# Bias rows of the first four heads made in their own partitions, and six early loads moved from GpSimd's queue to SyncE's

## The chip, the cores and the metric

The kernel runs on one core of a Trainium2 chip (the chip has eight). The metric is the device time of one execution in microseconds (us), the median of several runs. Five engines work side by side, each through its own list of instructions in order: TensorE (PE in the profile, with its weight loads as PEld), VectorE (DVE), ScalarE (ACT), GpSimd (POOL) and SyncE (SP). They wait for one another through semaphores. SP, ACT and POOL can issue DMA transfers; an engine that issues one spends time on the issue, and the transfer lands later.

## The reference, cut to what matters

Attention over 8 batches of 8 heads (64 heads, called head 0 to 63 here), 576 positions and head dimension 64, with a causal mask and a bias made of running sums of `s`; its output is the input of a gated feed-forward block.

```python
scores = scale * np.matmul(q, k.transpose(0, 1, 3, 2))
s_pos = np.maximum(s, 0.0)
cum = np.cumsum(s_pos, axis=-1)
bias = -(cum[:, :, :, None] - cum[:, :, None, :])
scores = np.where(causal, -1000000000.0, scores + np.minimum(bias, 0.0))
...                                   # softmax, then attn @ v gives x
g = x @ w_gate
silu = g * (1.0 / (1.0 + np.exp(-g)))
return (silu * (x @ w_val) @ w_out)   # 4608 tokens, 512 -> 1536 -> 512
```

The bias of position i against position j is `cum[j] - cum[i]`: a product of a column with ones. The kernel adds it inside the score product: beside the 64 rows of head dimension, an operand has extra rows that hold the running sum (in two parts, high and low, so that two 16-bit numbers carry it) and constants.

## The kernel before, in words

**Operands.** Four heads make a block (`HB`); block 0 is heads 0 to 3, block 1 heads 4 to 7. For a block there are two tiles `KQ[i][r]` (`kq` in the profile; `i` is the block modulo 2, `r` picks the pair of heads), 128 partitions by 2 sides (0 is q, 1 is k) by two heads of 576 columns and 64 columns of padding. For `r = 0`, partitions 0 to 63 hold the transposed head data and partitions 64 to 67 the bias rows, the rest of that half being zero; for `r = 1` the halves are swapped.

**Bias rows.** SP loads all 64 rows of `s` into `s_sb` (L188). DVE clips and scales it (L226), makes the running sum `c8` by a scan (L227), rounds it to 16 bits as the high part (L230), subtracts to get the low part (L231), and copies both parts for the other side (L232); the constant rows of the tile `HL` are filled by two memsets (L200, L201). `HL` has a partition for each head. The function `aug` (L183) then moves a head's four rows from its one partition of `HL` to four partitions of `kq` by a DMA, a DMA for each head, issued by SP for blocks 0 to 3.

**Head data.** `load_one` (L140) loads k or q as float32 (`rawk`, `rawq`); block 0 in two halves (`r = 0`, `r = 1`) by SP, blocks 1 and 2 whole by POOL. A cast to 16 bits (`ck`, `cq`) follows: L254 on ACT or L256 on POOL for the halves of block 0, L246 on DVE for block 1 and on POOL for block 2. PE transposes the cast data into a PSUM bank (L301 for halves, L287 for whole blocks), and L314 (ACT) or L316 (DVE) copies it from the bank to `kq`. V of batch 0 is loaded in five chunks by POOL (L157, `rawv`) and cast by POOL (four chunks, L168) and DVE (the last).

**Order of the start.** It is written out by hand at the end of the kernel and scheduled manually: each engine does its instructions in the order of the program text. `keep_warm` (L884) is a row of PE products whose result nobody reads: 32 at the start, 10 after the transposes of `r = 0`, 10 after those of `r = 1`. Then comes, in PE's order:

```python
        scores(0)
        half_batch("k")
        scores(1)
        half_batch("q")
        scores(2)
        scores(3)
```

`scores(h)` is `score_piece` for the four column chunks of head h: PE adds a mask product for the masked chunks (L353, `lower`) and the score products (L359), and ACT takes the exponential (L369) from the bank into `pt`. `half_batch(nm)` is the nine transposes (L287) of block 1's k or q, and the first four copies (L316) to `kq`. PE takes its products strictly in this order, so the products of head 1 stand behind the transposes of block 1's k, and those behind the cast of block 1's k.

**Banks.** PSUM has eight banks, handed out by `take` in a rotation fixed when the program is built; a product that opens a bank waits until the engine that read the bank last is done. The first piece of head 1 goes into bank 4, from which the last part of block 0's q (`r = 1`) is copied before.

**Later.** Heads 4 to 7, the products of the probabilities with V (L396, `values`), and then a loop over nine tiles of 512 tokens: gate and value products (L630), the down projection (L687, or by seven products instead of eight, L736), with the attention of the next batch pumped in between.

Of the kernel before, what the change touches and what calls it, by code (L numbers as in the profile page):

```python
# [12 lines left out]
FP32 = mybir.dt.float32  # L13
BF16 = mybir.dt.bfloat16
AF = mybir.ActivationFunctionType
ALU = mybir.AluOpType
# [3 lines left out]
def kernel(  # L20
# [43 lines left out]
    def pt_col(tj, bi):  # L64
# [4 lines left out]
    const = ctx.enter_context(tc.tile_pool(name="const", bufs=1))  # L69
# [21 lines left out]
    KQ = [  # L91
        [const.tile([128, 2, NR * S + 64], BF16, name=f"kq{e}{i}") for e in range(2)]
        for i in range(2)
    ]
    VT = [const.tile([128, NCH, H, D + 1], BF16, name=f"vt{i}") for i in range(2)]
    ident = const.tile([128, 128], BF16)
    one_s = const.tile([128, 1], FP32)
    HL = const.tile([BH, 4, 2, S], BF16)
    XR = 3 * TT
    XT = const.tile([128, 4, XR], BF16)  # L100
    warm = const.tile([128, 1], FP32)
    WS = const.tile([128, NFT // 2, 3, DM // 2], BF16)
    first_sbuf = ExitStack()
    first = first_sbuf.enter_context(tc.tile_pool(name="first", bufs=1))
    s_sb = first.tile([BH, S], FP32)
    c8 = first.tile([BH, S], FP32)
    PTP = {0: first, "bufs": 7}
    lower = first.tile([128, 512], BF16)

    with tc.manual_schedule():  # L110
# [50 lines left out]

        def cast_v(b, c, eng):
            n = 128 if c < 4 else TAIL
            dst, src_t = VT[b % 2][0:n, c, :, 0:D], loaded["v", b][0:n, c, :, :]
            if eng is nc.scalar:
                nc.scalar.copy(dst, src_t)
            else:
                eng.tensor_copy(dst, src_t)  # L168

        ONES2 = 1.0019378662109375  # L170
# [3 lines left out]
        def aug_rows(i, r):  # L174
            r0 = 64 * (1 - r)
            return KQ[i][r][r0 : r0 + 64, :, :].bitcast(FP32)

        def aug(hb, engs):
            for hh in range(HB):
                r, e = divmod(hh, 2)  # L180
                r0 = 64 * (1 - r)
                bh = hb * HB + hh
                engs[hh].dma_start(  # L183
                    KQ[hb % 2][r][r0 : r0 + 4, :, e * S : (e + 1) * S],
                    HL[bh : bh + 1, :, :, :],
                )
# [12 lines left out]
        nc.scalar.activation(warm, warm, AF.Exp)  # L199
        nc.vector.memset(HL[:, 0:2, 0, :].bitcast(FP32), ONES2)  # L200
        nc.vector.memset(HL[:, 2:4, 1, :].bitcast(FP32), NEGS2)  # L201
        make_identity(nc, ident)
        nc.gpsimd.memset(lower, 0.0)
        nc.gpsimd.affine_select(
# [3 lines left out]

        def pads(i):
            for r in range(2):  # L210
                nc.gpsimd.memset(KQ[i][r][64 * r : 64 * r + 64, :, NR * S :], 0.0)

        for r in range(2):
            nc.gpsimd.memset(aug_rows(0, r)[:, 1, :], 0.0)
# [4 lines left out]
        pads(0)  # L219
        nc.vector.memset(aug_rows(1, 0), 0.0)  # L220
        for nm in ("k", "q"):
            load_one(1, nm, eng=nc.gpsimd)
        init_vt(0)
        pads(1)

        nc.vector.tensor_scalar(s_sb, s_sb, 0.0, 8.0, ALU.max, ALU.mult)  # L226
        nc.vector.tensor_tensor_scan(  # L227
            c8, one_s[0:BH, 0:1].to_broadcast([BH, S]), s_sb, 0.0, ALU.mult, ALU.add
        )
        nc.vector.tensor_copy(HL[:, 0, 1, :], c8)  # L230
        nc.vector.tensor_sub(HL[:, 1, 1, :], c8, HL[:, 0, 1, :])  # L231
        nc.vector.tensor_copy(HL[:, 2:4, 0, :], HL[:, 0:2, 1, :])  # L232

        SP4 = [nc.sync] * 4
        GP4 = [nc.gpsimd] * 4
# [3 lines left out]
        def cast_one(hb, name, eng):  # L239
            cts[name, hb] = cp.tile([128, J, NR, D], BF16, tag="c" + name, bufs=2, name="c" + name)  # L240
            dst = cts[name, hb].rearrange("x j r d -> x r j d")
            src_t = loaded[name, hb]
            if eng is nc.scalar:
                nc.scalar.copy(dst, src_t)
            else:
                eng.tensor_copy(dst, src_t)  # L246

        def cast_half(hb, name, r, eng):
            if r == 0:
                cts[name, hb] = cp.tile([128, J, NR, D], BF16, tag="c" + name, bufs=2, name="c" + name)  # L250
            dst = cts[name, hb][:, :, r, :]
            src_t = loaded[name, hb][:, r, :, :]
            if eng is nc.scalar:
                nc.scalar.copy(dst, src_t)  # L254
            else:
                eng.tensor_copy(dst, src_t)  # L256
# [47 lines left out]

        def pe_out(hb, name, g, r, eng):
            j0, j1 = JG[g]
            kq = SRC[name][1]
            dst = KQ[hb % 2][r][64 * r : 64 * r + 64, kq, 0 : NR * S].rearrange(
                "a (x j) -> a x j", j=J
            )[:, :, j0:j1]  # L310
            tp = tps[name, g]
            srcp = tp[0][64 * r : 64 * r + 64].rearrange("a j x -> a x j")
            if eng is nc.scalar:
                nc.scalar.copy(dst, srcp)  # L314
            else:
                eng.tensor_copy(dst, srcp)  # L316
            tp[2] -= 1
            if tp[2] == 0:
                give(tp[1])
# [566 lines left out]
        def row_half(nm, r, eng):  # L886
            for g in range(2):
                pe_transpose_half(0, nm, g, r)
            for g in range(2):
                pe_out(0, nm, g, r, eng)  # L890

        def half_batch(nm):
            for g in range(2):
# [36 lines left out]
        w_load("v", 0, 1)  # L930
        for nm in ("g", "v"):
# [134 lines left out]
```

## Time and profile before

| what | us |
|---|---|
| median of three runs (376.23 to 377.41) | 376.51 |
| span of the profiled execution, first to last instruction | 375.9 |
| that execution's own time, its span with what lies around it: shown only through the runs | 376.23 to 377.41, so 0.3 to 1.5 around the span |
| PE busy | 364.4 (97%) |
| DVE busy | 290.4 (77%) |
| ACT busy | 240.3 (64%) |
| POOL busy | 212.1 (56%) |
| first score product (L359) | 12.65 |
| first exponential (L369) | 13.08 |

The mean granted PE clock is 1.000 over the span, and the clock row of the page shows 9 (90% or more) in each slice. By stages the PE is busy for 13.93 of the first 20 us, 38.82 of the next 40, and 311.67 of the last 315.9.

In the rows of the timeline the first number is the start in us from the span's start, the second the time that the merged instructions took, then engine, line, operation, what is written and what is read, shapes, and the count. A bracket gives the idle time before, and what ended it. In the rows by group the numbers behind the bar are the busy time in us, the mean in ns, and the idle time of the engine before them.

### The profile page before, as it was taken

How to read it: one execution, taken by the hardware profiler on the slowest of the kernel's cores; microseconds unless marked ns; L12 is line 12 of the kernel's file. 1: busy time of each engine (PE TensorE's matmuls, PEld its weight loads, DVE VectorE, ACT ScalarE, POOL GpSimd, SP SyncE). 2: the span in 40 equal slices, each digit the busy share in tenths (PEclk: the TensorE clock that was granted, in tenths of full speed). 3: DMA queues.
4: the chain of work that ended last, by engine and by line, in shares of the span. 5: the costliest groups of instructions: out<-in, count | busy, mean ns of one | idle time of the engine just before them, and what ended most of it. 6: DMA issues, size and time to landing. Idle time of an engine off the chain costs nothing.

```text
span 375.9 us, 8800 instructions
## 1 busy us (share of the span) xinstructions
PE 364.4 (97%) x3300; PEld 231.1 (61%) x3300; DVE 290.4 (77%) x578; ACT 240.3 (64%) x471; POOL 212.1 (56%) x325
## 2 busy tenths in 40 slices
PE   7699999999999999999999999999999999999995
PEld 6475556655555556855685558655865585476464
DVE  8867867458995899679976997599858867975984
ACT  8687777597986887578757876687465523323321
POOL 8982556665365657494649555955675416315320
PEclk9999999999999999999999999999999999999999
DMA  7899999799599998796869665995132103002003
GB/s 237 197 267 265 201 248 272 216 312 242 169 185 267 246 255 221 168 275 217 224 145 262 192 162 163 264 188 145 39 104 77 35 19 127 2 0 90 24 0 113
DMA packets 97146, 64.23 MB, mean 171 GB/s; under 512 B 77232, under 2 KB 82736, under 8 KB 97104
## 3 DMA queue, kind: packets, MB, share of 16 engines
q1 hardware_dynamic: 84976, 41.46, 45.9%
q0 software_dynamic: 12128, 22.21, 22.6%
q8 instruction: 26, 0.43, 0.5%
q14 instruction: 16, 0.13, 0.1%
HBM read 37.90 MB, written 19.86 MB: 154 GB/s over the span
## 4 chain that ended last, share of the span: by engine, by line
PE 90%; POOL 3%; ACT 2%; DVE 2%; DMA 1%; issue 1%; DVEq 0%; POOLq 0%; ACTq 0%
PE bank L630 47%; PE bank L736 17%; PE bank L359 11%; PE bank L396 8%; PE bank L687 6%; ACT pt L369 2%; DMA kq<-HL 1%; DVE kq L316 1%; PE bank L446 1%; DVE pp L653 1%; PE bank L287 1%; POOL vt L168 1%; DVE ht L664 1%; PE bank L353 1%; ACT kq L314 0%
## 5 line engine op out<-in xcount | busy, mean ns | idle before, releaser
L369 ACT ACTIVATE pt<-bank 128x512 bf16<-128x512 f32 (+1 forms) x256 | 120.3, 510 | 32.1 <-PE bank L359 18.9
L630 PE MATMUL bank<-XT,wg 128*128 128x512 bf16 x432 | 111.4, 379 | 0.5 <-DVE pp L653 0.3
L630 PE MATMUL bank<-XT,wv 128*128 128x512 bf16 x432 | 110.9, 379 | 0.1
L651 ACT ACTIVATE th<-bank 128x512 bf16<-128x512 f32 x108 | 64.7, 599 | 55.7 <-PE bank L630 51.1
L653 DVE SCALAR_TENSOR_TENSOR pp<-th,bank 128x512 bf16<-128x512 bf16 x108 | 73.7, 682 | 18.7 <-ACT th L651 18.2
L664 DVE SCALAR_TENSOR_TENSOR ht<-pp,bank 128x512 bf16<-128x512 bf16 x108 | 74.1, 687 | 10.6 <-PE bank L630 0.4
L359 PE MATMUL bank<-kq 128*128 128x128 bf16 (+4 forms) x576 | 75.8, 240 | 2.7 <-DMA kq<-HL 2.3
L673 POOL TENSOR_TENSOR ht<-ht 128x512 bf16<-128x512 bf16 x35 | 40.4, 1155 | 52.3 <-DVE su L671 52.2
L359 PEld LDWEIGHTS <-kq 128*128 128x128 bf16 x576 | 45.8, 98 | 33.1 <-DMA kq<-HL 2.6
L630 PEld LDWEIGHTS <-wv 128*128 128x128 bf16 x432 | 38.4, 98 | 36.4 <-issue 0.6
L630 PEld LDWEIGHTS <-wg 128*128 128x128 bf16 x432 | 38.3, 98 | 34.2 <-issue 0.7
L374 POOL TENSOR_SCALAR_AFFINE_SELECT pt<-pt 128x512 bf16<-128x512 bf16 x56 | 37.0, 661 | 30.8 <-ACT pt L369 23.4
L396 PEld LDWEIGHTS <-pt 128*128 128x128 bf16 x960 | 41.7, 98 | 17.3
L396 PE MATMUL bank<-vt,pt 128*128 128x65 bf16 x960 | 46.9, 194 | 0.3 <-POOL vt L168 0.3
L430 POOL DMA_DIRECT2D xs<-ot x24 | 21.7, 904 | 30.0 <-DVE ot L413 27.7
L736 PEld LDWEIGHTS <-ht 128*128 128x128 bf16 x336 | 31.2, 98 | 4.3
L413 DVE TENSOR_TENSOR ot<-bank,rc 128x320 bf16<-128x320 f32 x64 | 31.5, 492 | 2.2
L183 POOL DMA_DIRECT2D kq<-HL x48 | 28.7, 599 | 0.0
L687 PE MATMUL bank<-wo,ht 128*128 128x512 bf16 x96 | 25.8, 379 | 0.0
L736 PEld LDWEIGHTS <-su 128*128 128x128 bf16 x252 | 23.6, 98 | 3.3
L412 DVE RECIPROCAL rc<-bank 128x5 f32<-128x5 f32 x64 | 12.1, 189 | 15.3 <-PE bank L396 14.8
L801 POOL TENSOR_TENSOR ysb<-ysb 128x512 f32<-128x512 f32 x12 | 15.2, 1271 | 15.3 <-DVE ysb L795 15.3
(93 smaller groups left out, 389.1 us busy)
## 6 DMA issues: line engine op xcount, KB each, us to landing
out_dram<-ysb POOLq DMA_DIRECT2D x32, 256.0 KB, 3.9
rawv<-in_v_dram SPq DMA_DIRECT2D x28, 256.0 KB
rawk<-in_k_dram SPq DMA_DIRECT2D x12, 576.0 KB
rawq<-in_q_dram SPq DMA_DIRECT2D x12, 576.0 KB
xs<-ot POOLq DMA_DIRECT2D x24, 160.0 KB, 4.0
ks<-ck SPq DMA_DIRECT2D x11, 288.0 KB
qs<-cq SPq DMA_DIRECT2D x11, 288.0 KB
rawk<-in_k_dram POOLq DMA_DIRECT2D x3, 576.0 KB, 6.8
```

The source lines that it names most:

```text
L359: nc.tensor.matmul(sc[:, o : o + w], T[:, 1, e * S + 128 * tj : e * S + 128 * (tj + 1)], T[:, 0, e * S + lo : e * S + hi], start=not maske ...
L369: nc.scalar.activation(pt[:, c0 : c0 + n], sc, AF.Exp, scale=0.125)
L374: nc.gpsimd.affine_select(pt[:, 1088:1600], pt[:, 1088:1600], pattern=[[0, 4], [1, 128]], compare_op=ALU.is_ge, fill=zreg, base=0, channel ...
L396: nc.tensor.matmul(av[:, bi * (D + 1) : (bi + 1) * (D + 1)], pt[:, c0 : c0 + 128], VT[b % 2][:, tj, h, :], start=(tj == 0), stop=(tj == bi),)
L413: nc.vector.tensor_mul(ot[:, :, e * D : (e + 1) * D], av3[:, :, 0:D], rc[:, :, None].to_broadcast([128, NCH, D]),)
L630: nc.tensor.matmul(view(bs, TT), w[:, c, f0 : f0 + 128], xt[:, c, :], start=(c == 0), stop=(c == 3),)
L651: nc.scalar.activation(th, pg, AF.Tanh, scale=0.5)
L653: nc.vector.scalar_tensor_tensor(pp, in0=th, scalar=1.0, in1=pg, op0=ALU.add, op1=ALU.mult)
L664: nc.vector.scalar_tensor_tensor(hp[:, 2 * k2 : 2 * k2 + 2, :].rearrange("p a n -> p (a n)"), in0=pp, scalar=0.5, in1=pv, op0=ALU.mult, op ...
L673: (nc.vector if ft == NFT - 1 else nc.gpsimd).tensor_sub(hp[:, 1:3, :], hp[:, 1:4:2, :], hp[:, 0:3:2, :])
L687: nc.tensor.matmul(view(pys[ts_], DM), hps[ft // 2][:, 2 * (ft % 2) + half, c0 : c0 + 128], WO[j][:, ft % WKO, :], start=(ft == 0), stop=( ...
L736: nc.tensor.matmul(ps, lhs(p), rhs(p), start=(first and p == 0), stop=(last and p == NP - 1), skip_group_check=True,)
```

## The change

Diff, cut to its core. `...` marks what is left out.

```diff
-    HL = const.tile([BH, 4, 2, S], BF16)
+    HL = const.tile([128, 4, 2, S], BF16)
...
-    s_sb = first.tile([BH, S], FP32)
-    c8 = first.tile([BH, S], FP32)
+    s_sb = first.tile([128, S], FP32)
+    c8 = first.tile([128, S], FP32)
+    rows8 = first.tile([128, 8], FP32)
+    roles = first.tile([128, 4], FP32)
...
+        def hl_row(bh):
+            return bh + 4 if bh < 60 else bh + 64
...
-        nc.sync.dma_start(s_sb, s.rearrange("b h n -> (b h) n"))
+        s_copies(0, nc.sync)
+        s_copies(1, nc.scalar)
+        nc.scalar.dma_start(s_sb[8:64, :], s_rows[4:60, :])
+        nc.scalar.dma_start(s_sb[72:128, :], s_rows[8:64, :])
...
             load_one(0, "q", (r, r + 1))
+        load_qk(1)
...
-            nc.scalar.mul(
-                KQ[0][r][64 * (1 - r) : 64 * (1 - r) + 64, 0, :],
-                one_s[0:64, 0:1].to_broadcast([64, NR * S + 64]), 0.0,
-            )
...
-        for nm in ("k", "q"):
-            load_one(1, nm, eng=nc.gpsimd)
...
+        nc.vector.tensor_add(rows8, ident[:, 0:8], ident[:, 64:72])
+        nc.vector.tensor_add(roles, rows8[:, 0:4], rows8[:, 4:8])
+        nc.vector.tensor_reduce(a_q, roles[:, 0:2], axis=mybir.AxisListType.X, op=ALU.add, negate=True)
+        nc.vector.tensor_add(a_k, roles[:, 2:3], roles[:, 3:4])
+        nc.vector.tensor_reduce(b_lo, rows8[:, 0:4], axis=mybir.AxisListType.X, op=ALU.add)
+        nc.vector.tensor_scalar_add(b_lo, b_lo, -1.0)
...
         nc.vector.tensor_copy(HL[:, 0, 1, :], c8)
-        nc.vector.tensor_sub(HL[:, 1, 1, :], c8, HL[:, 0, 1, :])
-        nc.vector.tensor_copy(HL[:, 2:4, 0, :], HL[:, 0:2, 1, :])
+        nc.vector.scalar_tensor_tensor(
+            HL[:, 1, 1, :], in0=HL[:, 0, 1, :], scalar=b_lo, in1=c8,
+            op0=ALU.mult, op1=ALU.add,
+        )
+
+        def sums_rows(r, e, eng):
+            r0 = 64 * (1 - r)
+            for side, a, m in ((1, a_k, e), (0, a_q, 2 + e)):
+                eng.tensor_scalar(
+                    KQ[0][r][r0 : r0 + 64, side, e * S : (e + 1) * S],
+                    HL[r0 : r0 + 64, 1, 1, :], a[r0 : r0 + 64, :],
+                    roles[r0 : r0 + 64, m : m + 1], ALU.mult, ALU.add,
+                )
...
-        aug(0, SP4)
-        row_half("k", 0, nc.scalar)
-        row_half("q", 0, nc.vector)
-        cast_half(0, "k", 1, nc.scalar)
+        row_half("k", 0)
+        row_half("q", 0)
+        cast_half(0, "k", 1, nc.gpsimd)
         cast_half(0, "q", 1, nc.gpsimd)
-        nc.gpsimd.memset(aug_rows(1, 1), 0.0)
-        load_v(0, range(5), nc.gpsimd)
+        load_v(0, range(3))
+        nc.gpsimd.tensor_copy(HL[:, 2:4, 0, :], HL[:, 0:2, 1, :])
+        aug(1, SP4)
+        load_v(0, range(3, 5))
+        load_qk(2)
+        row_out("k", 0, nc.scalar, nc.scalar)
+        sums_rows(0, 0, nc.vector)
+        row_out("q", 0, nc.scalar, nc.vector)
+        row_half("k", 1)
+        row_half("q", 1)
+        sums_rows(0, 1, nc.vector)
+        for r, e in ((1, 0), (1, 1)):
+            sums_rows(r, e, nc.gpsimd)
+        row_out("k", 1, nc.vector, nc.vector)
+        row_out("q", 1, nc.vector, nc.vector)
         w_load("g", 0)
-        aug(1, SP4)
-        keep_warm(10)
-        row_half("k", 1, nc.scalar)
-        row_half("q", 1, nc.vector)
-        keep_warm(10)
-        cast_one(1, "k", nc.vector)
-        cast_one(1, "q", nc.vector)
-        for c in range(3):
+        cast_one(1, "k", nc.gpsimd)
+        cast_one(1, "q", nc.gpsimd)
+        for c in range(4):
             cast_v(0, c, nc.gpsimd)
-        load_one(2, "k", eng=nc.gpsimd)
-        cast_v(0, 3, nc.gpsimd)
-        load_one(2, "q", eng=nc.gpsimd)
...
         cast_v(0, 4, nc.vector)
+        for r in range(2):
+            nc.gpsimd.memset(KQ[0][r][64 * (1 - r) : 64 * (1 - r) + 64, 1, 0 : NR * S].bitcast(FP32), 0.0)
         aug(2, SP4)
```

What it does. `s` is loaded by four DMAs (one by SP, three by ACT) into 128 partitions: the partitions in which a bias row of heads 0 to 3 will stand get a copy of their head's row of `s` (`s_copies`, eight partitions for each pair of heads, four copies of two heads), and the other heads' rows fill the rest. The running sum is made in all 128 partitions at once. `b_lo` is 0 in the first four partitions of each such group of eight and -1 elsewhere, so that one instruction leaves the high part in some copies and the low part in others. For heads 0 to 3, `sums_rows` then writes the whole 64-partition half of `kq` by two instructions a head, each "the sum times a coefficient for this partition plus a constant for this partition"; the coefficients are zero where no row belongs. Heads 0 and 1 are done by DVE, heads 2 and 3 by POOL. Since the half is written whole, its zeroing for block 0 is dropped (ACT's two L215, POOL's two L214). The other blocks still get their rows by the DMA `aug`; the copy of `HL` to its other side goes from DVE to POOL. As eight rows of a half are in use for block 0 and four for block 2, POOL zeroes the k side again before `aug(2)`.

The moved work: the loads of k and q of block 1, of V of batch 0, and of k and q of block 2 are issued by SP instead of POOL, in the order shown, among the DMAs of `aug(1)`. The casts of k and q of block 1 go from DVE to POOL, behind the row instructions of heads 2 and 3 and the weight load `w_load("g", 0)`; the cast of the second half of block 0's k goes from ACT to POOL; the copies out of the banks for the second half of block 0 are all DVE's. The 20 later `keep_warm` products are removed. The order of `scores` and `half_batch` is as before.

More of the change, by code (lines that the diff above doesn't have):

```diff
@@ L104 @@
     first = first_sbuf.enter_context(tc.tile_pool(name="first", bufs=1))
-    s_sb = first.tile([BH, S], FP32)
-    c8 = first.tile([BH, S], FP32)
+    s_sb = first.tile([128, S], FP32)
+    c8 = first.tile([128, S], FP32)
+    rows8 = first.tile([128, 8], FP32)
+    roles = first.tile([128, 4], FP32)
+    a_q = first.tile([128, 1], FP32)
+    a_k = first.tile([128, 1], FP32)
+    b_lo = first.tile([128, 1], FP32)
     PTP = {0: first, "bufs": 7}
@@ L181, in aug, with s_copies @@
                 r0 = 64 * (1 - r)
-                bh = hb * HB + hh
+                row = hl_row(hb * HB + hh)
                 engs[hh].dma_start(
                     KQ[hb % 2][r][r0 : r0 + 4, :, e * S : (e + 1) * S],
-                    HL[bh : bh + 1, :, :, :],
+                    HL[row : row + 1, :, :, :],
                 )
-        nc.sync.dma_start(s_sb, s.rearrange("b h n -> (b h) n"))
+        s_rows = s.rearrange("b h n -> (b h) n")
+        def s_copies(r, eng):
+            r0 = 64 * (1 - r)
+            eng.dma_start(
+                s_sb[r0 : r0 + 8, :],
+                s_rows[None, 2 * r : 2 * r + 2, :].to_broadcast([4, 2, S]),
+            )
[3 more added lines that the diff above has]
+        nc.scalar.dma_start(s_sb[72:128, :], s_rows[8:64, :])
         def init_vt(i):
@@ L199 @@
         nc.scalar.activation(warm, warm, AF.Exp)
-        nc.vector.memset(HL[:, 0:2, 0, :].bitcast(FP32), ONES2)
-        nc.vector.memset(HL[:, 2:4, 1, :].bitcast(FP32), NEGS2)
+        nc.vector.memset(aug_rows(1, 0), 0.0)
         make_identity(nc, ident)
@@ L210, in pads @@
             for r in range(2):
-                nc.gpsimd.memset(KQ[i][r][64 * r : 64 * r + 64, :, NR * S :], 0.0)
+                nc.gpsimd.memset(KQ[i][r][:, :, NR * S :], 0.0)
+        pads(0)
+        init_vt(0)
+        nc.gpsimd.memset(aug_rows(1, 1), 0.0)
         for r in range(2):
-            nc.gpsimd.memset(aug_rows(0, r)[:, 1, :], 0.0)
-            nc.scalar.mul(
-                KQ[0][r][64 * (1 - r) : 64 * (1 - r) + 64, 0, :],
-                one_s[0:64, 0:1].to_broadcast([64, NR * S + 64]), 0.0,
-            )
@@ L219 @@
-        pads(0)
-        nc.vector.memset(aug_rows(1, 0), 0.0)
-        for nm in ("k", "q"):
-            load_one(1, nm, eng=nc.gpsimd)
-        init_vt(0)
-        pads(1)
+            nc.gpsimd.memset(KQ[1][r][64 * r : 64 * r + 64, :, NR * S :], 0.0)
+        nc.vector.tensor_add(rows8, ident[:, 0:8], ident[:, 64:72])
+        nc.vector.tensor_add(roles, rows8[:, 0:4], rows8[:, 4:8])
+        nc.vector.tensor_reduce(a_q, roles[:, 0:2], axis=mybir.AxisListType.X, op=ALU.add, negate=True)
+        nc.vector.tensor_add(a_k, roles[:, 2:3], roles[:, 3:4])
@@ L226 @@
+        nc.vector.tensor_reduce(b_lo, rows8[:, 0:4], axis=mybir.AxisListType.X, op=ALU.add)
+        nc.vector.tensor_scalar_add(b_lo, b_lo, -1.0)
+        nc.vector.memset(HL[:, 0:2, 0, :].bitcast(FP32), ONES2)
+        nc.vector.memset(HL[:, 2:4, 1, :].bitcast(FP32), NEGS2)
         nc.vector.tensor_scalar(s_sb, s_sb, 0.0, 8.0, ALU.max, ALU.mult)
         nc.vector.tensor_tensor_scan(
-            c8, one_s[0:BH, 0:1].to_broadcast([BH, S]), s_sb, 0.0, ALU.mult, ALU.add
+            c8, one_s[:, 0:1].to_broadcast([128, S]), s_sb, 0.0, ALU.mult, ALU.add
@@ L229 @@
         )
         nc.vector.tensor_copy(HL[:, 0, 1, :], c8)
-        nc.vector.tensor_sub(HL[:, 1, 1, :], c8, HL[:, 0, 1, :])
-        nc.vector.tensor_copy(HL[:, 2:4, 0, :], HL[:, 0:2, 1, :])
+        nc.vector.scalar_tensor_tensor(
[3 more added lines that the diff above has]
+        def sums_rows(r, e, eng):
+            r0 = 64 * (1 - r)
+            for side, a, m in ((1, a_k, e), (0, a_q, 2 + e)):
[3 more added lines that the diff above has]
+                    roles[r0 : r0 + 64, m : m + 1], ALU.mult, ALU.add,
+                )
@@ L884, in keep_warm, with row_half, row_out @@
                 nc.tensor.matmul(view(spare, 128), ident, ident, start=True, stop=True)
-        def row_half(nm, r, eng):
+        def row_half(nm, r):
             for g in range(2):
                 pe_transpose_half(0, nm, g, r)
+        def row_out(nm, r, *engs):
             for g in range(2):
-                pe_out(0, nm, g, r, eng)
+                pe_out(0, nm, g, r, engs[g])
         def half_batch(nm):
```

## Prediction

> **What bounds the kernel now.** I read the chain that ended last first: it tells whether a change of the first 20 us can reach the end at all.
>
> ```profile
> PE 90%; POOL 3%; ACT 2%; DVE 2%; DMA 1%; issue 1%; DVEq 0%; POOLq 0%; ACTq 0%
> ```
>
> The chain is PE's. The waits of PE by stages say the same more sharply: after 60 us there is none, and from 20 to 60 us these are all.
>
> ```profile
> PE bank L630 <- DVE pp L653: 0.3, 1, 0.3
> PE bank L359 <- DVE kq L316: 0.3, 1, 0.3
> PE bank L396 <- POOL vt L168: 0.3, 1, 0.3
> ```
>
> So from 20 us on PE works through its list with 0.9 us of waits, none of them on a load, and what the start gains or loses comes out at the end nearly one for one. Then the timeline of the start.
>
> ```profile
> 3.81 0.51 DVE L226 TENSOR_SCALAR s_sb<-s_sb 64x576 f32<-64x576 f32 x1 [0.25 <-DMA s_sb<-in_s_dram]
> ...
> 7.17 0.52 DVE L232 COPY HL<-HL 64x1152 bf16<-64x1152 bf16 x1
> ...
> 7.79 18.18 SPq L183 DMA_DIRECT2D kq<-HL  x16
> 7.99 0.66 POOL L256 CAST cq<-rawq 128x576 bf16<-128x576 f32 x1 [0.15 <-DMA rawq<-in_q_dram]
> ...
> 10.94 1.08 DVE L246 CAST ck<-rawk 128x1152 bf16<-128x1152 f32 x1 [0.27 <-DMA rawk<-in_k_dram]
> 12.43 0.76 DVE L246 CAST cq<-rawq 128x1152 bf16<-128x1152 f32 x1 [0.41 <-DMA rawq<-in_q_dram]
> ...
> 12.65 0.83 PE L359 MATMUL bank<-kq 128*128 128x128 bf16 x8 [2.28 <-DMA kq<-HL]
> 13.08 13.52 ACT L369 ACTIVATE pt<-bank 128x512 bf16<-128x512 f32 x32 [3.13 <-PE bank L359]
> ...
> 13.38 0.67 PE L287 MATMUL bank<-ident,ck 128*128 128x128 bf16 x9
> 13.82 0.10 PEld L353 LDWEIGHTS <-ident 128*128 128x128 bf16 x1
> 13.88 0.38 PE L353 MATMUL bank<-lower,ident 128*128 128x512 bf16 x1
> ```
>
> Head 0 waits for its bias rows: they are ready at 7.69, and the first row DMA, issued at 7.79, lands at 12.6. From 13.08 ACT is the bound: 32 exponentials in 13.52 us, 1.69 a head, to 26.6. Head 1's mask product starts at 13.88, its first exponential when head 0's are done (13.08 + 1.69 = 14.77). Block 1's k, transposed between heads 0 and 1, has been cast at 10.94 + 1.08 = 12.02, so no one waits for it.
>
> **The change part by part.**
>
> *Bias rows of head 0.* The last copy of `s` is ACT's third issue: SP's rows give about 0.58 an issue, so it starts at 0.82 + 2 x 0.58 = 1.98; the load of before took 3.81 - 0.82 = 2.99 from issue to use; it lands near 5.0. Six small DVE operations (0.19 each by the reciprocal of five elements) and the memsets lie before that, hidden. From clip to the second part DVE took 7.13 - 3.81 = 3.32, and partitions cost nothing: the sum is ready at 8.3. Two row operations follow. Bounds: half of L232 (0.26) and all of L226 (0.51); I take 0.3, nearest to L232, which is 16-bit too. With one copy of q (0.72, from L316) head 0's operand is whole at 8.3 + 0.6 + 0.72 = 9.6, and after four transposes and the mask product its scores start near 10.4 and its exponentials near 10.8: 2.3 earlier than before. The row DMAs of heads 0 to 3 and their 4.81 us of wait are gone.
>
> *What is late next.* Head 1's products stand in PE's order behind the transposes of block 1's k, whose cast now stands on POOL. POOL's list: its memsets end near 6.1; the second half of q lands as before and is cast by 7.99 + 0.66 = 8.65 (the half of k before it, 0.66, fits: it arrives first). Then:
> - the copy of `HL`, 128x1152: 1.14, as POOL's L246 with as many elements (lower bound DVE's 0.52);
> - four row operations of 64x576. No row shows one on POOL. Below: 0.26, half of DVE's copy. Above: 1155 ns of L673 (two tensors, 512 elements) x 576/512 = 1.30. Nearest is L374, one 16-bit tensor with a rule per element: 661 x 576/512 = 0.74. Four: 2.96;
> - the issue of the gate weights, 0.78 (L332);
> - the cast of k, 1.14; and about 0.3 of gaps, seven of 0.04 to 0.05.
>
> ```profile
> L673 POOL TENSOR_TENSOR ht<-ht 128x512 bf16<-128x512 bf16 x35 | 40.4, 1155 | 52.3 <-DVE su L671 52.2
> L374 POOL TENSOR_SCALAR_AFFINE_SELECT pt<-pt 128x512 bf16<-128x512 bf16 x56 | 37.0, 661 | 30.8 <-ACT pt L369 23.4 <-issue 6.6
> ...
> L246 POOL CAST ck<-rawk 128x1152 bf16<-128x1152 f32 x4 | 4.6, 1140 | 2.0 <-DMA rawk<-in_k_dram 2.0
> ```
>
> Sum 1.14 + 2.96 + 0.78 + 1.14 + 0.3 = 6.32, so the cast ends at 8.65 + 6.32 = 15.0, and the transposes start there instead of at 13.38: 1.6 to 1.7 late. Head 1's exponential comes 1.2 after them (transposes, mask product, four score products): 16.2 instead of 14.77, **1.4 to 1.5 late**. ACT has done head 0 by 12.5 and then stands idle; the 2.3 us won for head 0 are not passed on. The cast of q ends 1.2 after that of k, PE needs it after head 1's products (1.4 to 1.6): hidden, as is everything that follows at the old distance.
>
> *DVE's list.* Sums of heads 0 and 1 and five copies: 8.3 + 0.6 + 0.72 + 0.6 + 4 x 0.72 = 13.1, when bank 4 is free for head 1 (mask product at 13.88 before). That is hidden behind POOL by 15.0 + 0.5; if POOL were fast, this would set head 1, at best 0.8 us earlier than before.
>
> *DVE beside POOL.* L246 shows one shape at 1081 ns while POOL issued V's DMAs, and at 761 ns after: 0.3 us from company. I leave 0.3 to the range. The Trainium skill, page "SBUF — State Buffer", section "SBUF: two separate sides", is harsher and speaks against this change: GpSimd and a two-port DVE operation exclude each other for a whole instruction. By that rule each of DVE's four row operations could wait out one POOL operation, an estimate of 1.14 + 3 x 0.74 = 3.4 us, bank 4 free at 16.5 and the kernel near 379; the row here, 0.3, is why I do not count it.
>
> *Loads moved to SP.* POOL loses nine issues, 0.91 + 0.74 + 4.72 + 0.71 + 0.73 = 7.8 us up to 19.4; the row instructions, casts and copy put back 1.14 + 2.96 + 2.28 + 0.66 = 7.0, of which 6.2 stand before the cast of k. SP issues in 0.43 to 0.6 each and waits on landings of earlier loads; block 1's loads go out near 4, no later than POOL's (4.42, 5.33), so they land by 12.4 as before. `aug(1)` then goes out near 9.8 behind three chunks of V, and four issues of 0.62 plus 4.81 end near 17; head 4 needs it about 20.8 (19.35 before): 4 us of cover, beyond which each us costs one. V is cast on POOL from 16.2 to 18.7 and first used at 21.3 + 1.4: hidden. k and q of block 2, cast at 24.31 before, have time. Two memsets before `aug(2)` (0.6 each, L214) fall near 23, for head 8 at about 40: hidden.
>
> *Removed.* ACT's two L215 (2.45), POOL's two L214 (1.25) and 20 filler products (1.46 by their rows) all ended before the 12.65 at which the row DMA let PE go: nothing by themselves. On the fillers: PE stood idle for 2.28 us before 12.65, and its next eight products took 0.83, as those at 14.09 (0.82), so such a gap costs nothing here. After the change the longest gap, from head 0's end near 12.2 to 15.0, is 2.8. The skill's page "TensorE: Matmul & The Clock Gate", section "What's actually happening", has the clock halved after an idle window of about 3.4 us that runs freely; no run here shows a gap of that length. By it a POOL list one us longer than mine would cost another estimated 1 us.
>
> *Sum.* The profiled execution spans 375.9, and the runs' median of 376.5 lies 0.6 above. Span 375.9 + 1.5 = 377.4; time **376.5 + 1.5 = 378.0**.
>
> **The rivals.**
> - *The forecast: POOL's cast of block 1's k sets head 1*, with row operations at 0.6 to 0.9. The range of this case is 377.2 to 379.0. Half of the chances, most of them above the line of 0.3% (1.13 us, about what a measurement can tell from no change), a fifth of them below.
> - *Dear POOL or the port:* row operations at 1.30 add 4 x 0.56 = 2.2, waits between DVE and POOL up to 1, a later `s` 0.5: 379.0 to 381.7. For it: L673's price, and the 1081 against 761. Against: these operations read one tensor. 15%.
> - *POOL and DVE meet:* copy at 0.52 and row operations at 0.45 end the cast near 13.2; DVE's bank 4 at 13.1. Gain and loss cancel: 375.4 to 377.2. 23%.
> - *Faster:* one mechanism, the missing row DMA is passed on. That needs both lists done by 12.5: POOL's copy at 0.52 and rows at 0.26 give 8.65 + 0.52 + 1.04 + 0.78 + 1.14 + 0.3 = 12.4, and DVE's bank 4 must come with an `s` that lands at 4.4 instead of 5.0. Head 1 then starts at 12.6 instead of 13.88, 1.3 less: 375.2, at most 374.7. It decides the sign from where the cast ends before 13.4 and bank 4 is free before 13.8. Against: no row shows POOL at half DVE's price. 12%.
>
> **How the numbers follow.** Of the meeting case 0.03 spills over the lines, 0.02 above and 0.01 below. Slower: 0.5 x 0.8 + 0.15 + 0.02 = 0.57; same: 0.5 x 0.2 + 0.20 = 0.30; faster: 0.12 + 0.01 = 0.13. The range, 375.3 to 380.2, leaves out the far half of the dear case and most of the faster one.
>
> **What would show it.** The first L391 product (L359 of before) near 10.4 without a DMA in front; the POOL row operations L260 at 0.74; POOL's cast of `ck` ending near 15; PE idle for about 2.8 us in front of L319, put down to POOL; ACT idle between 12.5 and 16, then busy to 28. I am wrong if PE's gap is elsewhere, if L260 on POOL takes under 0.5 or over 1, or if DVE's copies end after 15.

## The result, and the profile after

The changed kernel takes 390.55 us (median of four runs, 389.69 to 391.87) against 376.62 in the same session (four runs, 376.23 to 377.41): a ratio of 1.037, 95% interval [1.034, 1.039]. The forecast was 378.0, with a range of 375.3 to 380.2. The sign was right, the size wrong by 12.5 us.

I read the chain that ended last first. Its shares by engine, from the page of the changed kernel:

```profile
PE 81%; DVE 9%; DMA 3%; issue 2%; ACT 1%; POOL 1%; ACTq 0%; DVEq 0%
```

PE has 81% of it instead of 90%, DVE 9% instead of 2%: of a span of 389.4 us, some 27 us more lie on DVE. The waits of PE from 20 to 60 us say where to look (columns: waiter, whom it waited for, total us, times, longest).

```profile
PE bank L385 <- DVE kq L348: 6.3, 1, 6.3
...
PE bank L428 <- DVE vt L173: 0.4, 1, 0.4
```

PE's gap is there, but behind DVE and inside head 0, not behind POOL's cast of k. The timelines of DVE and of POOL show why; the second number of a row is the time it took.

```profile
7.51 0.46 DVE L247 TENSOR_SCALAR s_sb<-s_sb 128x576 f32<-128x576 f32 x1 [3.02 <-DMA s_sb<-in_s_dram]
8.01 1.81 DVE L248 TENSOR_TENSOR_SCAN c<-one_s,s_sb 128x576 f32<-128x576 f32 x1
...
11.49 1.33 DVE L260 TENSOR_SCALAR kq<-HL,a_k,roles 64x576 bf16<-64x576 bf16 x1
12.74 0.42 DVE L260 TENSOR_SCALAR kq<-HL,a_q,roles 64x576 bf16<-64x576 bf16 x1
13.20 0.71 DVE L348 COPY kq<-bank 64x512 bf16<-64x512 bf16 x1
13.95 7.16 DVE L260 TENSOR_SCALAR kq<-HL,a_k,roles 64x576 bf16<-64x576 bf16 x1
21.03 0.71 DVE L260 TENSOR_SCALAR kq<-HL,a_q,roles 64x576 bf16<-64x576 bf16 x1
```

```profile
11.52 1.15 POOL L948 COPY HL<-HL 128x1152 bf16<-128x1152 bf16 x1 [1.23 <-DVE HL L252]
12.65 1.04 POOL L260 TENSOR_SCALAR kq<-HL,a_k,roles 64x576 bf16<-64x576 bf16 x1
13.70 0.81 POOL L260 TENSOR_SCALAR kq<-HL,a_q,roles 64x576 bf16<-64x576 bf16 x1
14.50 0.81 POOL L260 TENSOR_SCALAR kq<-HL,a_k,roles 64x576 bf16<-64x576 bf16 x1
15.30 0.81 POOL L260 TENSOR_SCALAR kq<-HL,a_q,roles 64x576 bf16<-64x576 bf16 x1
16.07 0.97 POOL L364 DMA_DIRECT2D wg<-in_moe_w_gate_dram  x1
17.04 1.16 POOL L278 CAST ck<-rawk 128x1152 bf16<-128x1152 f32 x1
18.13 1.15 POOL L278 CAST cq<-rawq 128x1152 bf16<-128x1152 f32 x1
19.22 2.36 POOL L173 CAST vt<-rawv 128x512 bf16<-128x512 f32 x4
```

Four DVE row operations of one form and one shape (L260) took 1.33, 0.42, 7.16 and 0.71 us, while POOL works from 11.52 to 21.58 with no pause. DVE's copies for head 0 and head 1 are queued behind the 7.16. Two smaller things: the clip of `s` starts at 7.51 (3.81 before) after a wait for the load; and three of POOL's four row operations take 0.81, the first 1.04, and the cast of k ends at 18.20.

**A common yardstick.** Gate products begin only after the whole start, so the start of the first activation on them (`th`, 32.13 in the kernel before) measures what the start lost; the last of the 108 (361.81) shows what the end keeps. The table holds every run; the experiments follow.

| kernel | median us | ratio, interval | first `th` late | last `th` late |
|---|---|---|---|---|
| changed | 390.55 | 1.037 [1.034, 1.039] | 12.34 | 13.58 |
| e1_order | 385.57 | 1.022 [1.014, 1.029] | 7.23 | 7.39 |
| e2_rows_act | 384.10 | 1.018 [1.011, 1.024] | 5.85 | 6.17 |
| e3_fillers | 389.71 | 1.033 [1.025, 1.040] | 11.44 | 11.63 |
| e4_loads_only | 381.19 | 1.012 [1.007, 1.017] | 3.11 | 3.29 |
| e5_k1q1_sp | 378.68 | 1.004 [1.002, 1.006] | -1.50 | 0.30 |
| e6_s_first | 383.40 | 1.017 [1.010, 1.024] | 3.67 | 3.97 |
| e7_casts_dve | 381.74 | 1.012 [1.007, 1.018] | 2.81 | 3.11 |
| e8_rows_before_v | 382.32 | 1.016 [1.010, 1.021] | 6.41 | 7.98 |
| e9_k_cast_early | 381.70 | 1.013 [1.009, 1.017] | 2.96 | 5.50 |
| e10_longer_list | 389.20 | 1.034 [1.031, 1.037] | 9.50 | 9.68 |
| e11_kq_casts_early | 380.21 | 1.011 [1.007, 1.015] | 0.03 | 1.63 |
| e12_after_again | 390.28 (one run) | | 11.95 | 12.70 |

Lateness is that of the profiled execution, the median that of all runs; the two can differ by a us or two. One of e5's ten runs took 1350 us; it is in the median, not in the ratio.

### The profile page after: what moved, and what is told of

It reads as the page before. It is cut to its first block, busy times and chain, and to the rows that moved or that the text cites. A ratio compares the mean times of both kernels' runs of the same rounds, so it can differ in the third digit from the quotient of the medians.

```text
span 389.4 us, 8727 instructions
## 1 busy us (share of the span) xinstructions
PE 365.3 (94%) x3239; PEld 232.9 (60%) x3280; DVE 302.0 (78%) x586; ACT 237.0 (61%) x467; POOL 211.9 (54%) x324
## 4 chain that ended last, share of the span: by engine, by line
PE 81%; DVE 9%; DMA 3%; issue 2%; ACT 1%; POOL 1%; ACTq 0%; DVEq 0%
PE bank L662 42%; PE bank L768 16%; PE bank L391 9%; PE bank L428 7%; PE bank L719 5%; DVE kq L348 3%; DVE kq L260 2%; DMA pk<-ks 2%; DMA s_sb<-in_s_dram 1%; DVE pp L685 1%; DVE ht L696 1%; PE bank L478 1%; ACT pt L401 1%; DVE vt L173 1%; PE bank L319 1%
## 5 line engine op out<-in xcount | busy, mean ns | idle before, releaser
L662 PE MATMUL bank<-XT,wv 128*128 128x512 bf16 x412 | 109.3, 379 | 1.1
L391 PE MATMUL bank<-kq 128*128 128x128 bf16 (+4 forms) x576 | 77.3, 244 | 0.8 <-issue 0.3
L391 PEld LDWEIGHTS <-kq 128*128 128x128 bf16 x576 | 46.9, 100 | 37.8 <-issue 9.9
L719 PE MATMUL bank<-wo,ht 128*128 128x512 bf16 x90 | 24.8, 379 | 0.3
L411 POOL TENSOR_SCALAR_AFFINE_SELECT pt<-pt 128x64 bf16<-128x64 bf16 x56 | 14.6, 261 | 18.5 <-ACT pt L401 18.3
```

The costliest lines, as they stand in the source:

```text
L391: nc.tensor.matmul(sc[:, o : o + w], T[:, 1, e * S + 128 * tj : e * S + 128 * (tj + 1)], T[:, 0, e * S + lo : e * S + hi], start=not maske ...
L662: nc.tensor.matmul(view(bs, TT), w[:, c, f0 : f0 + 128], xt[:, c, :], start=(c == 0), stop=(c == 3),)
L719: nc.tensor.matmul(view(pys[ts_], DM), hps[ft // 2][:, 2 * (ft % 2) + half, c0 : c0 + 128], WO[j][:, ft % WKO, :], start=(ft == 0), stop=( ...
```

## The experiments

Theory P: DVE's row operation and POOL's instructions exclude each other (the port of the prediction's second case), and DVE waits out POOL's list. Rivals: the row operation is dear by itself; the loads moved to SP; the fillers' removal and the clock; the late `s`; POOL's list, as forecast.

**e1: DVE's four row operations first, POOL's behind them.** POOL's rows read copies of the coefficients that DVE writes after its own rows, so POOL waits.

```diff
         sums_rows(0, 0, nc.vector)
+        sums_rows(0, 1, nc.vector)
+        nc.vector.tensor_copy(a_kp, a_k)
+        nc.vector.tensor_copy(a_qp, a_q)
...
-            for side, a, m in ((1, a_k, e), (0, a_q, 2 + e)):
+            for side, a, m in ((1, (a_k, a_kp)[r], e), (0, (a_q, a_qp)[r], 2 + e)):
...
-        sums_rows(0, 1, nc.vector)
         for r, e in ((1, 0), (1, 1)):
             sums_rows(r, e, nc.gpsimd)
+        nc.gpsimd.tensor_copy(HL[:, 2:4, 0, :], HL[:, 0:2, 1, :])
```

> Heads 0 and 1's four row operations stand first on DVE, and POOL's list (rows of heads 2 and 3, then the HL copy, the weight issue, the casts) starts only when they are done, through two small copies of their coefficients. Theory P (port): a DVE row operation cannot get in while POOL works without a pause; DVE's four rows then take about 0.42 us each, none 7.16, head 1's mask product comes near 20.7 instead of 24.64, and the time is about 386.5. Rival S (slow operation): the row operation is slow on DVE by itself; a row of several us stays, POOL starts later still, and the time is 391 or more.

Measured on DVE's timeline of e1:

```profile
11.52 0.43 DVE L262 TENSOR_SCALAR kq<-HL,a_k,roles 64x576 bf16<-64x576 bf16 x1
11.87 0.44 DVE L262 TENSOR_SCALAR kq<-HL,a_q,roles 64x576 bf16<-64x576 bf16 x1
12.20 0.45 DVE L262 TENSOR_SCALAR kq<-HL,a_k,roles 64x576 bf16<-64x576 bf16 x1
12.54 0.45 DVE L262 TENSOR_SCALAR kq<-HL,a_q,roles 64x576 bf16<-64x576 bf16 x1
```

The same operations took 1.77 us in sum against 9.62. The row operation is not dear by itself; its company is. Head 1's mask product came at 20.69, as expected, and the time falls by 5 us although POOL's list starts later.

**e2: the rows of heads 0 and 1 on ACT**, as `activation(Identity)` with a scale and a bias for each partition; nothing else is changed.

```diff
...
-        sums_rows(0, 0, nc.vector)
         row_out("q", 0, nc.scalar, nc.vector)
+        sums_rows(0, 0, nc.scalar)
...
-        sums_rows(0, 1, nc.vector)
+        sums_rows(0, 1, nc.scalar)
```

> Heads 0 and 1's four row operations go from DVE to ACT, which is idle there; all else as after. Theory P: DVE is left with copies out of PSUM, no wait of several us on it, ACT's rows 0.7 each; POOL's cast of block 1's k, ending near 17, sets head 1; mask product of head 1 near 17.7 instead of 24.64, time about 383.5. Rival S: ACT's rows are as slow as DVE's were, time 388 or more. Rival C (clock): the half clock is what costs, time 389 to 391.

The ACT rows took 0.84 to 0.86, and 12.34 of lateness became 5.85: **6.5 us are the row operation's stall**, with what followed from it (head 1's mask product alone came 5.45 earlier, at 19.19 instead of 24.64). Behind it comes what the prediction had put first, PE waiting for POOL's cast of k, in e2's timeline:

```profile
13.22 0.84 ACT L262 ACTIVATE kq<-HL,roles,a_k 64x576 bf16<-64x576 bf16 x1
...
18.25 1.14 PE L326 MATMUL bank<-ident,ck 128*128 128x128 bf16 x9 [3.35 <-POOL ck L285]
```

**e3: fillers put back** into the gaps, three times 16 and 100 within head 0.

```diff
         row_half("k", 0)
+        keep_warm(16)
         row_half("q", 0)
+        keep_warm(16)
...
+        keep_warm(16)
         row_half("q", 1)
...
+        keep_warm(100)                       # before head 0's last piece
```

> The change with 148 filler products put back into TensorE's gaps before and within head 0. Theory P: the 7.16 us row stays, only the half clock between 7.7 and 28.2 us goes; the four runs of after that differ in their granted clock put that at 1.7, so about 389. Rival C: with the clock whole most of the 14 us go, time 380 or less.

The row operation took 7.16 again; 0.9 of lateness went, of which 0.3 had gone before that operation began. So the clock is not the main cause. How much it costs this run does not say, for the fillers kept only head 0's products at the full rate (eight took 0.82); head 1's ran at about half of it, as in the changed kernel:

```profile
24.73 1.48 PE L391 MATMUL bank<-kq 128*128 128x128 bf16 x8
```

**e4: the kernel before with all nine moved loads on SP and nothing else.**

```diff
+        load_qk(1)                           # SP, before s is used
...
-        load_v(0, range(5), nc.gpsimd)
+        load_v(0, range(3))                  # SP
         w_load("g", 0)
         aug(1, SP4)
+        load_v(0, range(3, 5))
+        load_qk(2)
```

> The kernel before with nothing but the moved loads: k, q of blocks 1 and 2 and V of batch 0 issued by SP. Theory P: no part in the loss; the row DMA of head 0 sees less or as much traffic, time 376.0 to 377.5. Rival L (loads): SP's queue is the loss, the row DMAs wait behind the loads and the time is 379 or more.

Theory P's number was missed and the rival's held. Head 0 comes earlier (products at 10.99 instead of 12.65), but head 4 waits for its row DMA, which SP issued only at 15.96, behind V:

```profile
10.38 5.54 SPq L157 DMA_DIRECT2D rawv<-in_v_dram  x3
15.96 3.92 SPq L183 DMA_DIRECT2D kq<-HL  x4
```

```profile
20.69 1.44 PE L358 MATMUL bank<-kq 128*128 128x128 bf16 x8 [2.62 <-DMA kq<-HL]
```

The three issues of V hold SP for 5.54 us. In the changed kernel `aug(1)` went out at 12.69, ahead of V's last two chunks, and no wait of PE for a row DMA shows, so this loss is no part of the 12.34.

**e8: as e4, with `aug(1)` ahead of V.**

```diff
-        load_v(0, range(3))
         w_load("g", 0)
         aug(1, SP4)
-        load_v(0, range(3, 5))
+        load_v(0, range(5))
```

> The kernel before with all the loads moved to SP, but the row DMAs of block 1 ahead of V in SP's queue. If the place of the row DMAs behind V's loads was what cost the earlier run 4 us, head 4 no longer waits (20.69 there, about 17.7 here) and the time is 375 to 376.5. Rival: V itself lands late on SP's queue, POOL's casts of V still wait some us, and the time is 378 or more.

Now V is late: POOL waits 8.2 us for the first chunk, PE 2.5 and 2.1 for the casts. The expected time was missed again, and again on the rival's side: on SP's queue either the rows or V come late in the kernel before. This profiled execution was the longest of its runs.

**e5: the kernel before with only block 1's k and q on SP.**

```diff
             load_one(0, "q", (r, r + 1))
+        load_qk(1)
...
-        for nm in ("k", "q"):
-            load_one(1, nm, eng=nc.gpsimd)
```

> The kernel before with only the loads of k and q of block 1 moved to SP, right behind those of block 0; V and block 2 stay on POOL, the bias rows as before. In the run with all loads moved, head 0's products started at 10.99 instead of 12.65 and head 1's at 12.22 instead of 13.88; the loss came later, from V and the row DMAs of block 1. If the early part is the loads of block 1 alone, head 0 starts near 11.0 here too, nothing comes later, and the time is 1.2 to 1.7 below the kernel before, near 375.3. Rival: the row DMA was early only because V was not yet under way; then it lands at 12.6 as before and the time is that of before.

The start gained 1.50 us and kept it up to 133 us; at the end 0.30 were lost. The median is 1.65 above that of the kernel before in its session (377.03); the profiled execution shows 0.30 of that, and the rest stays open. Between the same activations the lead falls by 0.57 at 137 us, 0.18 by 160 and 1.08 at 300. The last step in e5's timeline:

```profile
296.35 0.89 POOL L429 DMA_DIRECT2D xs<-ot  x1 [4.08 <-DVE pp L652]
...
299.07 0.36 PE L395 MATMUL bank<-vt,pt 128*128 128x65 bf16 x6 [0.90 <-DVE ht L663]
```

`ot` was written at 294.48, so this POOL issue began 1.87 us after its data, when a DVE operation ended; in the kernel before it began 0.30 after (295.25 to 295.55). POOL's tensor operation and mask came late behind it, and PE waited. What held the issue the profile does not show. Just before the first, PE waits 0.41 for `ot` at 134; the changed kernel has the same step (0.57, with the same wait) and two more (0.20 and 0.48 by 255), which are its 13.58 - 12.34.

**e6: e2, with the large copies of `s` issued first.**

```diff
-        s_copies(0, nc.sync)
-        s_copies(1, nc.scalar)
-        nc.scalar.dma_start(s_sb[8:64, :], s_rows[4:60, :])
+        nc.sync.dma_start(s_sb[8:64, :], s_rows[4:60, :])
         nc.scalar.dma_start(s_sb[72:128, :], s_rows[8:64, :])
+        s_copies(0, nc.sync)
+        s_copies(1, nc.scalar)
```

> Rows of heads 0 and 1 on ACT, as in the run before, and the two large copies of s issued first, each ahead of everything on its queue. Theory: the clip waits for the third issue on ACT's queue (issued at 2.51, landed at 7.4 behind the loads of k and q); issued at 0.82 it lands near 5.3, the whole chain to POOL's cast of block 1's k moves up by 2, head 1's mask product to 17.2, the time to about 382. Rival: the small broadcast copies or the traffic itself set it; then s lands after 6.5 and the time stays within 0.7 of 384.1.

The clip started at 5.41 instead of 7.72, and POOL's list at 9.37; the cast of k ended 6.45 later, at 15.82. Lateness fell by 2.18. The median moved less than the profiled execution (two runs, 381.91 and 384.89): 0.70, within the spread of the two.

**e7: e6, with block 1's casts back on DVE and 48 fillers** (e3's three `keep_warm(16)`).

```diff
-        cast_one(1, "k", nc.gpsimd)
-        cast_one(1, "q", nc.gpsimd)
+        cast_one(1, "k", nc.vector)
+        cast_one(1, "q", nc.vector)
```

> As the run with s first, with the casts of block 1's k and q back on DVE and 48 fillers on TensorE. Theory P (port): the casts read and write SBUF only, so they wait like the row operations did while POOL works through its copy, rows and weight issue; the first cast takes well over 0.76 us and ends only near the end of that list, about 15, and head 1 starts near 16, time about 380.5. Rival: a cast from float32 is not kept out; it ends near 13.9, head 1 starts at 14.5, time 378.5.

Neither theory was put to the test: the cast of k began only at 14.97, behind DVE's own copies, which the fillers had made late, when POOL's rows were done.

```profile
11.86 3.08 DVE L355 COPY kq<-bank 64x640 bf16<-64x640 bf16 x4 [0.97 <-PE bank L340]
14.97 1.29 DVE L285 CAST ck<-rawk 128x1152 bf16<-128x1152 f32 x1
```

DVE's casts took 1.29 and 1.72 (0.76 with POOL idle, in e4) beside POOL's casts of V. Eight products took 0.82 to 0.87 throughout, and head 1's lateness of 2.95 did not grow (2.81 at the first `th`); in e6, where head 1's eight took 1.48, 2.54 became 3.67.

**e9: e6, with POOL's cast of k ahead of its row operations; e11: the casts of k and of q.**

```diff
+        cast_one(1, "k", nc.gpsimd)
+        cast_one(1, "q", nc.gpsimd)          # e11; in e9 behind the rows
         for r, e in ((1, 0), (1, 1)):
             sums_rows(r, e, nc.gpsimd)
...
-        cast_one(1, "k", nc.gpsimd)
-        cast_one(1, "q", nc.gpsimd)
```

> On top of the run with rows of heads 0 and 1 on ACT and the large copies of s first: POOL casts block 1's k straight after the copy of HL, then makes the four rows of heads 2 and 3, then casts q. The cast of k should end near 11.7 (15.82 in that run), so head 1's mask product starts near 13 instead of 16.42 and PE has no gap of 4 us, so no half clock. Theory V (behind POOL's list the next late thing is V, whose last two loads SP issues only behind aug(1): they landed near 23.2 in that run, first use 24.94 against 21.27 before): the values of heads 0 and 1 still start near 24.5 to 25, and the time is 379.5 to 380.5. Rival (V is not a bound, POOL's list was the whole rest of the loss): the values start near 20.5 to 21.3 and the time is 375.5 to 376.5.

Head 1's mask product came at 12.90, a us earlier than before the change. V was not the bound: its casts ran from 17.23 without a wait, so theory V fell, though the values started at 24.42, near what it said; the time, 381.70, lies outside both forecasts. What came in its place is the wait for the cast of q and then the half rate, in e9's timeline of PE:

```profile
16.36 0.68 PE L326 MATMUL bank<-ident,cq 128*128 128x128 bf16 x9 [2.11 <-POOL cq L285]
...
19.03 1.48 PE L398 MATMUL bank<-kq 128*128 128x128 bf16 x8
```

Behind the start this execution lost another 2.54, in steps from 137 to 255 us.

> As the run before with the early cast of k, with the cast of q early too: POOL copies HL, casts block 1's k and q (to end near 13.1), then makes the rows of heads 2 and 3 (to end near 16.4). In the run before, head 1's mask product came at 12.90 (13.88 in the kernel before), but the transposes of q waited 2.1 us for a cast that ended at 16.30, PE fell to half clock from about 17.5 to 24.4, and the values of heads 0 and 1 started at 24.42. Theory L (POOL's list, then the clock that the gap brings, were what was left): without the gap PE keeps full clock, the values start near 20.3 to 21, the first gate product is level with or up to 1 us ahead of the kernel before, and the time is 375.3 to 377. Rival (the clock falls without that gap, since the fillers are gone, or the rows of head 2 are the next late thing): the values start after 22.5 and the time is 378 or more.

The start is level, as theory L has it: the values began at 21.29 (21.27 before), and eight products took 0.82 to 0.88 from 13.74 on.

```profile
13.74 0.88 PE L398 MATMUL bank<-kq 128*128 128x128 bf16 x8
...
21.29 1.08 PE L435 MATMUL bank<-vt,pt 128*128 128x65 bf16 x30
```

So the rest of the start's loss was POOL's list and the gap it made. The total is not level, and theory L's time was missed: the median is 380.21 (378.82 to 383.44, six runs), and its profiled execution of 379.52 loses 1.3 near 57 us, where POOL waits 1.7 for a chunk of V of the next batch and PE 1.2 for POOL's cast. The longer executions of e11 were not profiled; what they lose stays open.

**e10: the changed kernel with two more POOL casts of q** (the same tile written again) ahead of the casts of V.

```diff
         cast_one(1, "q", nc.gpsimd)
+        for again in range(2):
+            nc.gpsimd.tensor_copy(cts["q", 1].rearrange("x j r d -> x r j d"), loaded["q", 1])
```

> The changed kernel with two more POOL casts of block 1's q (written again to the same tile, 1.15 us each) between its cast of q and the casts of V; nothing on PE's path waits for them. Theory P (DVE's row operation is kept out as long as POOL's instructions follow one another): the row operation that took 7.16 us takes 9.3 to 9.6, ends near 23.4 instead of 21.1, and the time rises by about 2.3, to 392.5 or 393. Rival (the row operation waits for one thing at a fixed place, the weights' DMA issue at 16.07 or the casts of k and q that end at 19.28, or is slow in itself): it still takes 7.0 to 7.3 us and the time stays near 390.5.

Both failed. On e10's timelines of DVE and of POOL:

```profile
13.74 2.34 DVE L260 TENSOR_SCALAR kq<-HL,a_k,roles 64x576 bf16<-64x576 bf16 x1
16.00 3.26 DVE L260 TENSOR_SCALAR kq<-HL,a_q,roles 64x576 bf16<-64x576 bf16 x1
```

```profile
15.87 0.97 POOL L364 DMA_DIRECT2D wg<-in_moe_w_gate_dram  x1
...
19.15 2.37 POOL L966 CAST cq<-rawq 128x1152 bf16<-128x1152 f32 x2
```

Neither operation waited out the list. The first ended at 16.08, 0.2 after POOL's DMA issue began (15.87); the second at 19.26, just past a break between two POOL casts (19.09 to 19.15). In the changed kernel the 7.16 ended at 21.11, 0.2 after the last cast of V began (20.89), and that cast took 0.69 where its three fellows took 0.61 to 0.62; the 1.33 at 11.49 ended at 12.82, 0.17 after POOL's first row operation began, the one that took 1.04 instead of 0.81. So in these runs a DVE row operation got in only where one POOL instruction gives way to the next, and not at each such place: at the ninth in the changed kernel, at the third, twice, in e10.

**e12: the changed kernel once more.**

> The changed kernel itself once more, on this chip, for a second profile of it. In the run with the longer list DVE's row operation of head 1 got in at the third start of a POOL instruction, in the changed kernel's first profile only at the ninth. Theory D (where it gets in is fixed by the program): the row operation takes 7.1 to 7.2 us again and the time is 389.5 to 392. Theory C (it is chance, execution by execution): it takes another time, ending with the start of another POOL instruction (near 2.3, 3.3, 4.3, 5.4 or 6 us), and the time moves with it, down to 385.

```profile
13.84 7.17 DVE L260 TENSOR_SCALAR kq<-HL,a_k,roles 64x576 bf16<-64x576 bf16 x1
```

It took 7.17, again to the ninth start, as in the first profile and in e3, whose list is the same: theory D's numbers were met. Chance is not excluded by that. Up to the third start e10's list is that of the changed kernel, with the same distances to 0.01 us, and DVE's operation begins 0.25 behind a POOL row operation in both; yet in e10 it got in there, before the lists differ. What decides the place is open. This execution also bears on the clock: the record of the granted clock is 1.00 from 5 to 35 us, where the first profile has 0.50 from 10 to 25, and yet eight products took 1.49 us in both, and the first `th` is 0.39 apart. On this kernel the rate of like products told the state of PE, the record did not.

## Why the prediction was wrong

**The step that failed** is "DVE beside POOL": "I leave 0.3 to the range", and "the row here, 0.3, is why I do not count it". DVE's row operations of heads 0 and 1 took 9.62 us instead of the 1.77 they take alone: 7.85 of company, of which 6.49 reach the first `th` (12.34 - 5.85). The row that I weighed, 1081 ns against 761, I also misread: both casts, at 10.94 and at 12.43, ran while POOL issued V's DMAs, the second not after them.

```profile
9.64 4.72 POOL L157 DMA_DIRECT2D rawv<-in_v_dram  x5
```

It was not DVE in company against DVE alone, and it said nothing of POOL's twelve instructions in a row from 11.52 to 21.58. The Trainium skill, page "SBUF — State Buffer", section "Who interferes with whom", says that an operation like these in a two-port mode and GpSimd exclude each other for a whole instruction. The runs agree with that in so far as DVE waits and POOL goes on; in which mode these operations ran, no run shows. I set the rule aside for one mild row. My estimate by the rule, 3.4, was short as well, because I let DVE wait for one POOL operation each time; the runs show it passed over at eight starts in a row.

**`s` "lands near 5.0".** The clip waited until 7.51. ACT's first issue, the broadcast, took 1.25 instead of my 0.58, so the last large copy was issued at 2.51 instead of 1.98; and from there to its use it took 5.0 instead of the 2.99 of the kernel before, for which no run gives the reason. With the large copies issued first, `s` was in use at 5.41 (e6), which was worth 2.18 of lateness. The sum then took 3.94 instead of 3.32, with the scan at 1.81, begun just behind a POOL cast (1.36 in e1 and e6, where no cast was ahead of it).

**POOL's list, 6.32 to the end of the cast of k.** It measured 6.68 (11.52 to 18.20), and 6.45 in e6; row operations took 0.81 against 0.74. It began at 11.52 instead of 8.65, since the sum was late. This mechanism was right and nearly rightly sized: without the stall and the late `s`, head 1's mask product was 2.54 late (e6) where I had 1.6 to 1.7, and the first `th` 3.67, of which a part is the half rate. Taking it away (e9, then e11) removed 3.64.

**Fillers "nothing by themselves".** The rate does count once PE has gaps: a lateness of 2.54 became 3.67 in e6 at about half rate, while at full rate 2.95 stayed 2.81 in e7, which has 48 fillers but also other casts, so the fillers' share is not shown apart. I had ranked the gap by length. In the kernel before 2.28 us cost nothing, in e9 the products had slowed after 2.11. The skill's page "TensorE: Matmul & The Clock Gate", section "What's actually happening", puts the clock to a free-running activity window of about 3.4 us. Both gaps are shorter than that, and the slower rate followed the shorter of them, so the length of the gap alone does not give the rate here; no run separates such a window from the missing fillers.

**Loads on SP "hidden".** This held: neither in the changed kernel nor in e11, whose start is level, does PE wait in the start for a load that was moved. It depends on what else SP issues: in the kernel before, with the row DMAs of heads 0 to 3 on the same queue, the same loads cost 3.1 (e4) or 6.4 (e8). They are nine, not the six of the title; and of the 7.0 us put back on POOL, 5.9 stand up to the end of the cast of k by the terms given there, not 6.2.

**"What the start gains or loses comes out at the end nearly one for one."** A loss did, 12.34 becoming 13.58. A gain didn't: -1.50 became +0.30 (e5). The forecast's faster rival leaned on that sentence.

The sum of the start's loss, by the ladder changed, e2, e6, e9, e11: 6.49 stall, 2.18 late `s`, 0.71 cast of k, 2.93 cast of q with the half rate, 0.03 left. That makes 12.34; another 1.24 are the late steps. This is the ladder of single profiled executions, in this order of steps; by the medians of all runs its steps are 6.45, 0.70, 1.70 and 1.49, so only the first is clear of the spread of the runs. No version beat the kernel before.

## What to carry to other kernels

Before work is put on POOL, ask which DVE operations will run beside the whole list, and allow them a wait of up to that list (7.16 us here), not that of one mild row; order (DVE first) or another engine takes the price away. A transfer that feeds the first chain goes out first, ahead of small and broadcast ones. A gain at the start is worth only what the later hand-overs between engines let through, so look for the lead at several places of the span, not at its start alone.

## What the hardware showed that I had not expected

- A DVE operation of 0.43 us was kept waiting for 7.16 beside back-to-back POOL instructions, at the same start of theirs in three profiles, and for 2.34 in a fourth with the same list up to there; DVE's copies from a PSUM bank beside them took their usual 0.71.
- It goes both ways, by who begins first: DVE's scan, begun 0.06 behind a POOL cast, took 1.81, and POOL's next half cast beside it 1.66 (0.66 before); in e1 the scan began 0.10 ahead of POOL's cast, kept its 1.36, and that cast took 1.71. The row operation at 11.49 does not fit this: it began 0.03 ahead of POOL's copy and still took 1.33.
- The broadcast loads of `s` (18 KB) cost 0.76 to 1.25 us to issue on ACT, in the changed kernel and e6; the seven times larger plain ones 0.37 to 0.66.
- Eight products took 1.49 us at a recorded clock of 1.00 (e12), where the kernel before took 0.82 to 0.87.
